# Turned tokens copied behind a block's last first product, gating in one Silu pass, and a moved step of weight additions

## The chip, the cores and the metric

The kernel runs on one core of one Trainium2 chip. The metric is the device time of one execution in microseconds. The engines are named as in the profile: PE (matmuls; PEld its weight loads), DVE (vector engine), ACT (activations and copies), POOL (the general engine), and SP (issues most transfers). Each works through its own instructions in order and waits on the others by semaphores.

## The reference, cut to what matters

Three stages follow one another: pooled attention, a mixture of experts with a skip score, and a dense feed-forward stage with a SiLU gate. The change lies in the last one and in the last expert work ahead of it.

```python
def _moe2_ref(x, w_in, w_out):          # x: 4608 x 512, w_in: 512 x 2048, w_out: 2048 x 512
    h = x @ w_in
    g = h * (1.0 / (1.0 + np.exp(-h)))
    return (g @ w_out).astype(np.float32)
```

## The kernel before, in words

Every fp32 operand of a matmul is split into a high half and a low half (a rounded copy, made by ACT, and what is left of it, a subtraction on DVE or POOL). A product is high x high, high x low and low x high, so 12 matmuls of 128x512 make one 128x512 product over a depth of 512.

The 4608 tokens of the feed-forward stage are nine blocks of 512. Three blocks are done plainly, in four **visits** (`visits` in `ffn`): visit 0 takes the first block with the hidden slices f = 0 to 5 (`HALF` = 6), visit 1 the second block with f = 0 to 15, visit 2 the first block again with f = 6 to 15, and visit 3 the third block with f = 0 to 15. The other six blocks are done in pairs by Strassen's scheme, in 24 steps n (`strassen(n)`, then `second(n - 1)`).

Inside a visit PE's order is `mm1(0)`, `mm1(1)`, `mm2(0)`, `mm1(2)`, `mm2(1)`, and so on: `mm1(f)` is the **first product** (into the PSUM tile `fh`), `mm2(f)` the **second product** (into `fop`). At a visit's end `mm2(last)` follows `mm2(last - 1)` with no first product between, and then the next visit's `mm1(0)` comes. Between `mm1(f)` and `mm2(f)` stand: a Sigmoid on ACT (`fsg`), a multiplication on DVE (`fsg` again), the high half on ACT (`fgh`), and the low half on DVE (`fgl`). The second product uses `fgh` in its first 8 matmuls and `fgl` in its last 4; the last one of a visit asks for `fgl` in every third.

The tokens of a block reach PE like this. `load_x` has SP load them into `fx` (four transfers), `turn(b, k)` transposes quarter k on DVE into `xt` (k = 0 to 3), and `xtrans(b, k)` splits `xt` into the halves of `xth` and `xtl` (ACT copies, DVE subtracts). Both halves lie in the tile `w1l`, which the profile therefore names; the last expert's first products read the same tile. So `xtrans` of a block can only run once all first products of the block ahead are done. For the first block the same is done out of `raw1` by way of `xn`, inside `moe`, between the last expert unit's second products (`yp`). This place is called the **handover** here.

Beside this, DVE decodes the weights of later slices (`convert`, up to three of its steps behind each first product, by the list `PACE`; DVE names `ft`, `fr`), ACT and POOL split them (`fh`, `fl`), and only then SP loads the next raw weights (`fr`). In visits 2 and 3 a generator `adds` makes the sums of weights that Strassen's scheme needs: per pair of slices one step of six POOL additions (`sw`), and one step with an ACT copy and a POOL subtraction (`shl`). One step is put behind each first product.

What fixes the order on an engine is the order of the calls in the code; no scheduler moves them. Every instruction goes through a helper at L115, so all have that line in the profile and are told apart by their tiles.

## Time and profile before

| | us |
|---|---|
| median of 3 runs | 1280.05 |
| lowest and highest of the 3 | 1272.41, 1280.28 |
| the profiled execution: its time | 1275.63 |
| the profiled execution: span from first to last instruction | 1273.9 |
| PE busy | 1227.5 |
| DVE busy | 874.7 |
| ACT busy | 565.7 |
| POOL busy | 357.0 |

The feed-forward stage begins at 504 us of the span and fills the rest. A matmul's end is modelled in the profile, so the busy share of PE says little; what PE loses is read from the starts: matmuls that follow each other at a steady distance lose nothing, and a larger distance is a wait. The profiled execution took 1.7 us more than its span, and lies between the three timed runs.

### The profile page before, as it was taken

The page shows a single profiled execution, that of the slowest core. Times are in us where ns is not written, and L with a number is a line of the kernel's source. Part 1 is how long each engine was busy: PE and PEld are TensorE (multiplying, and loading weights), DVE is VectorE, ACT ScalarE, POOL GpSimd, SP SyncE. Part 2 cuts the span into 40 slices and gives each one's busy share as a digit, 9 for nine tenths or more (in the row PEclk, how much of TensorE's full clock was granted, in tenths as well). Part 3 has the DMA queues.
Part 4 walks back from the last instruction along what each step waited for, and adds up shares of the span by engine and source line. Part 5 has one row for each costly group of instructions (what it writes and reads, how often), then busy time and mean ns, then how long its engine had stood idle before and what let it go on. Part 6 is the DMA issues. An engine that isn't in the chain of part 4 may idle for free.

```text
span 1273.9 us, 19902 instructions
## 1 busy us (share of the span) xinstructions
PE 1227.5 (96%) x6309; PEld 1041.7 (82%) x6310; DVE 874.7 (69%) x1599; ACT 565.7 (44%) x1200; POOL 357.0 (28%) x313
## 2 busy tenths in 40 slices
PE   6999898999999989999999999999999999999998
PEld 5988778998788977788887887788888888888887
DVE  6888876676776768899725365657785577846565
ACT  5877534455554544444433225433444233442321
POOL 5477532132222321322376512110201011110100
PEclk9999999999999999999999999999999999999999
DMA  9988536565666634568672435572565644362532
GB/s 374 327 300 290 193 104 242 172 199 179 236 211 207 192 109 116 141 177 296 237 238 110 132 91 131 192 205 101 182 172 200 163 143 155 137 228 93 180 118 89
DMA packets 110509, 234.45 MB, mean 184 GB/s; under 512 B 15525, under 2 KB 48421, under 8 KB 106720
## 3 DMA queue, kind: packets, MB, share of 16 engines
q1 hardware_dynamic: 103136, 216.47, 51.8%
q0 software_dynamic: 7008, 16.80, 4.2%
q8 instruction: 42, 0.69, 0.2%
q14 instruction: 35, 0.29, 0.1%
q10 hardware_dynamic: 288, 0.20, 0.1%
HBM read 183.24 MB, written 52.89 MB: 185 GB/s over the span
## 4 chain that ended last, share of the span: by engine, by line
PE 58%; DVE 3%; DMA 1%; ACT 1%; issue 0%; SPq 0%; DVEq 0%; ACTq 0%
PE yb L115 20%; PE ps L115 17%; PE fh L115 9%; PE fop L115 9%; PE hp L115 1%; DVE w1l L115 1%; DMA fx<-xa 1%; DMA wout<-wdo 0%; DVE st L115 0%; PE yp L115 0%; DVE xcb L115 0%; DVE fr L115 0%; DMA out<-fo 0%; DVE fsg L115 0%; ACT fgh L115 0%
## 5 line engine op out<-in xcount | busy, mean ns | idle before, releaser
L115 PE MATMUL yb<-wout,g 128*128 128x512 f32 x1152 | 265.3, 389 | 1.1 <-DMA wout<-wdo 1.1
L115 PEld LDWEIGHTS yb<-wout,g 128*128 128x128 f32 x1152 | 216.1, 188 | 46.6 <-DMA wout<-wdo 1.9
L115 POOL TENSOR_TENSOR tm<-tm,tm 128x512 f32<-128x512 f32 x24 | 32.2, 1340 | 404.8 <-ACT tm L115 404.8
L115 DVE TENSOR_TENSOR yacc<-yb,yacc 128x512 f32<-128x512 f32 x168 | 115.5, 687 | 29.0 <-PE yb L115 23.3
L115 ACT COPY tm<-ps 128x512 f32<-128x512 f32 x72 | 42.3, 587 | 142.7 <-PE ps L115 139.7
L115 ACT CAST g<-sg 128x512 fp32r<-128x512 f32 x96 | 59.7, 622 | 81.4 <-DVE sg L115 81.4
L115 PE MATMUL fh<-w1l,fh 128*128 128x512 f32 x336 | 85.5, 394 | 5.7 <-DVE w1l L115 3.0
L115 DVE TENSOR_TENSOR w2l<-raw,w2h 128x512 fp32r<-128x512 f32 x96 | 65.8, 690 | 28.8 <-ACT w2h L115 24.7
L115 ACT ACTIVATE hh<-hp 128x256 fp32r<-128x256 f32 (+1 forms) x96 | 39.4, 410 | 99.0 <-PE hp L115 88.3
L115 DVE TENSOR_TENSOR tm<-ps,tm 128x512 f32<-128x512 f32 x24 | 16.6, 691 | 97.3 <-PE ps L115 97.3
L115 PE MATMUL yp<-w2h,hh 128*128 128x512 f32 x208 | 82.9, 399 | 0.1
L115 PE MATMUL yp<-w2l,hh 128*128 128x512 f32 x208 | 81.2, 391 | 1.5 <-DVE w2l L115 1.5
L115 PE MATMUL yp<-w2h,hl 128*128 128x512 f32 x208 | 81.3, 391 | 0.0
L115 PEld LDWEIGHTS fh<-w1l,fh 128*128 128x128 f32 x336 | 63.6, 190 | 20.6 <-DVE w1l L115 4.1
L115 PE MATMUL hp<-xth,w1h 128*128 128x256 f32 (+2 forms) x384 | 72.3, 309 | 7.5 <-PEq L1663 3.6
L115 DVE TENSOR_TENSOR fsg<-fh,fsg 128x512 f32<-128x512 f32 x48 | 32.9, 686 | 67.6 <-ACT fsg L115 67.6
L115 PE MATMUL hp<-xtl,w1h 128*128 128x256 f32 (+2 forms) x384 | 72.4, 309 | 3.1 <-DVE xtl L115 1.9
L115 ACT ACTIVATE fsg<-fh 128x512 f32<-128x512 f32 x48 | 28.7, 598 | 96.1 <-PE fh L115 96.1
L115 PE MATMUL hp<-xth,w1l 128*128 128x256 f32 (+2 forms) x384 | 71.1, 308 | 0.0
L115 ACT ACTIVATE prb<-s,mx 128x72 f32<-128x72 f32 x288 | 65.3, 355 | 10.4 <-DVE mx L115 10.4
L115 DVE TENSOR_TENSOR g<-sg,g 128x512 fp32r<-128x512 f32 x96 | 65.7, 685 | 5.2 <-ACT g L115 4.7
L115 PEld LDWEIGHTS hp<-xth,w1h 128*128 128x128 f32 x384 | 60.1, 191 | 10.3 <-issue 8.7
(235 smaller groups left out, 2735.6 us busy)
## 6 DMA issues: line engine op xcount, KB each, us to landing
raw<-w SPq DMA_DIRECT2D x88, 512.0 KB, 4.8
wout<-wdo SPq DMA_DIRECT2D x48, 512.0 KB
win<-wdi SPq DMA_DIRECT2D x36, 512.0 KB
w1l<-wdi SPq DMA_DIRECT2D x36, 512.0 KB
xa<-x SPq DMA_DIRECT2D x36, 256.0 KB
fx<-xa SPq DMA_DIRECT2D x36, 256.0 KB
v<-vR SPq DMA_DIRECT2D x7, 1280.0 KB
fr<-w_in SPq DMA_DIRECT2D x16, 512.0 KB
```

The source lines that it names most:

```text
L115: ins = f(*a, **k)
```

## The change

It has three parts.

1. **Turned tokens.** At the end of a visit, quarters 0 and 1 of the next block are turned one first product earlier than before (behind the third-last, not the second-last), and quarters 2 and 3 too (behind the second-last, not the last). All four are split right behind the last first product; before, two were split there and two between the matmuls of the visit's last second product. At the handover the four quarters are turned and split ahead of the second products' evictions, through three buffers in place of two.
2. **Gating.** The Sigmoid on ACT and the multiplication on DVE become one Silu on ACT, in the visits (48 times) and in Strassen's steps (4 per step, 96 times).
3. **Additions.** `adds` takes no step behind the last first product of visit 2, and two steps behind the third one of visits 2 and 3. `PACE` gets one more entry, a 0 for the last slice of visit 1.

```diff
--- before.py
+++ after.py
@@ -45,7 +45,7 @@
 DEEP = 3
 LOW1 = 30, 31, 32, 35
 FMIN = float(np.uint32(0x38100000).view(np.float32))
-PACE = [3, 3, 3, 3, 1, 0] + [3, 2, 3] * 5
+PACE = [3, 3, 3, 3, 1, 0] + [3, 2, 3] * 5 + [0]
 HALF = 6
 POOL = 8
 PAD = 352
@@ -1066,19 +1066,18 @@
                 some(OPS[f // 2])
             gt = gates()
             one = s1.tile([1, 1], F32, name="one", tag="one")
-            nc.scalar.activation(one, gt[0:1, 0:1], AF.Sigmoid)
+            nc.scalar.activation(one, gt[0:1, 0:1], AF.Silu)
             sc = None
 
-            def xtrans(ks):
-                for k in ks:
-                    o = xn[:, k % 2, 0:DM]
-                    self.turn(o, x, k)
-                    self.split(self.fxh[:, k], self.fxl[:, k], o)
+            for k in range(5):
+                if k < 4:
+                    self.turn(xn[:, k % U, 0:DM], x, k)
+                if k:
+                    self.split(self.fxh[:, k - 1], self.fxl[:, k - 1], xn[:, (k - 1) % U, 0:DM])
 
             for s in (2, 1):
                 mm2(s, gt)
                 sc = scatter(s, sc, self.sq)
-                xtrans((4 - 2 * s, 5 - 2 * s))
                 while done:
                     f = done.pop(0)
                     self.ffn_conv3(f)
@@ -1213,8 +1212,7 @@
                         nc.tensor.matmul(ps, w[:, 0, P * k:P * (k + 1)], x[:, k], start=(i == 0), stop=(i == 11))
                         i += 1
                 sg = s2.tile([P, 512], F32, name=f"fsg{b}_{f}", tag="fsg")
-                nc.scalar.activation(sg, ps, AF.Sigmoid)
-                nc.vector.tensor_tensor(sg, ps, sg, ALU.mult)
+                nc.scalar.activation(sg, ps, AF.Silu)
                 gh = s2.tile([P, 512], F32R, name=f"fgh{b}_{f}", tag="fgh")
                 gl = s2.tile([P, 512], F32R, name=f"fgl{b}_{f}", tag="fgl")
                 nc.scalar.copy(gh, sg)
@@ -1227,7 +1225,7 @@
                     next(conv, None)
                 return gh, gl
 
-            def mm2(f, g, ops, fs, between=None):
+            def mm2(f, g, ops, fs):
                 h, l = self.fw[f]
                 gh, gl = g
                 last = f == fs[-1]
@@ -1237,8 +1235,6 @@
                                      start=(first and f == fs[0]), stop=(stop and last))
 
                 for s in range(4):
-                    if between and s in (1, 2):
-                        between(s + 1)
                     mm(s, gh, h, first=True)
                     mm(s, gh, l)
                     if last:
@@ -1410,10 +1406,7 @@
 
                 def sig(j, h):
                     sg[j] = s2.tile([P, DM], F32, name=f"sg{n}_{j}", tag="fgl" if j == 1 else "fsg")
-                    nc.scalar.activation(sg[j], h, AF.Sigmoid)
-
-                def gate(j, h):
-                    nc.vector.tensor_tensor(sg[j], h, sg[j], ALU.mult)
+                    nc.scalar.activation(sg[j], h, AF.Silu)
 
                 def high(j):
                     g[j] = slot(18 + 4 * (n % 2) + j, F32R, f"g{n}_{j}")
@@ -1441,33 +1434,23 @@
                 early(2)
                 prod(pa, a12, "b21", False)
                 sig(0, pa)
-                gate(0, pa)
                 prod(pb, s_4, "b22", False)
                 sig(3, h22)
                 h12 = h(1, "fgh")
                 nc.vector.tensor_tensor(h12, pb, p1, ALU.add)
                 high(0)
                 low(0)
-                gate(3, h22)
                 prod(pc, a22, "t4", False)
                 h21 = h(2, "fgl")
                 nc.vector.tensor_tensor(h21, pc, p1, ALU.add)
                 sig(1, h12)
                 high(3)
 
-                def t0():
-                    gate(1, h12)
-                    sig(2, h21)
-
                 def t1():
                     low(3)
                     high(1)
 
-                def t2():
-                    gate(2, h21)
-                    high(2)
-
-                return [t0, t1, t2, lambda: low(1), lambda: low(2)]
+                return [lambda: sig(2, h21), t1, lambda: high(2), lambda: low(1), lambda: low(2)]
 
             ring = [0]
 
@@ -1509,21 +1492,22 @@
                 for f in fs:
                     g[f] = mm1(b, f, pace.pop(0) if pace else 2)
                     if v >= 2:
-                        next(adds, None)
+                        for _ in range(0 if f == fs[-1] and v == 2 else 2 if f == fs[0] + 2 else 1):
+                            next(adds, None)
                     if v >= 1 and f > fs[0] + 2:
                         for k in [next(keeps, None)]:
                             if k is not None:
                                 self.ffn_keep(k)
                     if f == fs[0] + 2:
                         load_x(after if after is not None else doubles[0][0])
-                    if after is not None and fs[-1] - f in (0, 1):
-                        for k in (2, 3) if f == fs[-1] else (0, 1):
+                    if after is not None and fs[-1] - f in (1, 2):
+                        for k in (2, 3) if f == fs[-1] - 1 else (0, 1):
                             turn(after, k)
                     if f == fs[0] + 4 and fs[0] > 0:
                         load_part()
                     if f == fs[-1] and after is not None:
-                        xtrans(after, 0)
-                        xtrans(after, 1)
+                        for k in range(4):
+                            xtrans(after, k)
                     if f > fs[0]:
                         mm2(f - 1, g.pop(f - 1), ops, fs)
                     if after is None:
@@ -1550,7 +1534,7 @@
                     load_in(1)
                     tail = strassen(0)
                     load_x(doubles[1][0])
-                mm2(fs[-1], g.pop(fs[-1]), ops, fs, (lambda k: xtrans(after, k)) if after is not None else None)
+                mm2(fs[-1], g.pop(fs[-1]), ops, fs)
                 store(b, ops, fs)
             load_out(0)
 
```

DVE at the handover (`gt` is the gate of the last expert unit, `x_84<-yp` its evictions, `raw_79` the loaded tokens, `xn` the turned ones, `w1l` their low half, `fr_2602` raw weights), before:

```order
L115 RECIPROCAL gt<-gt 128x3
L115 SCALAR_TENSOR_TENSOR x_84<-yp_3694,gt,xr 128x512
L115 STREAM_TRANSPOSE xn<-raw_79 128x512
L115 TENSOR_TENSOR w1l<-xn,w1l 128x512
L115 STREAM_TRANSPOSE xn<-raw_79 128x512
L115 TENSOR_TENSOR w1l<-xn,w1l 128x512
L115 SCALAR_TENSOR_TENSOR raw_79<-fr_2602,raw_79 128x1024
L115 SCALAR_TENSOR_TENSOR fr_2602<-fr_2602,raw_79 128x1024
L115 SCALAR_TENSOR_TENSOR fr_2602<-raw_79,fr_2602 128x1024
L115 SCALAR_TENSOR_TENSOR x_84<-yp_3737,gt,xr 128x512
L115 STREAM_TRANSPOSE xn<-raw_79 128x512
L115 TENSOR_TENSOR w1l<-xn,w1l 128x512
```

and now:

```order
L115 RECIPROCAL gt<-gt 128x3
L115 STREAM_TRANSPOSE xn<-raw_79 128x512 x2
L115 TENSOR_TENSOR w1l<-xn,w1l 128x512
L115 STREAM_TRANSPOSE xn<-raw_79 128x512
L115 TENSOR_TENSOR w1l<-xn,w1l 128x512
L115 STREAM_TRANSPOSE xn<-raw_79 128x512
L115 TENSOR_TENSOR w1l<-xn,w1l 128x512 x2
L115 SCALAR_TENSOR_TENSOR x_84<-yp_3706,gt,xr 128x512
L115 SCALAR_TENSOR_TENSOR raw_79<-fr_2602,raw_79 128x1024
L115 SCALAR_TENSOR_TENSOR fr_2602<-fr_2602,raw_79 128x1024
L115 SCALAR_TENSOR_TENSOR fr_2602<-raw_79,fr_2602 128x1024
L115 SCALAR_TENSOR_TENSOR x_84<-yp_3743,gt,xr 128x512
```

The four turns and the four subtractions now stand ahead of the first eviction; before, two of each stood behind it, and two behind the second.

DVE at the end of visit 0 (the first number in `fgl_4_...` is f, that in `xt_0_...` is k), before:

```order
L115 SCALAR_TENSOR_TENSOR fr_3774<-fm,fr_3774 128x1024
L115 TENSOR_TENSOR fsg_4_4000<-fh_4_3987,fsg_4_4000 128x512
L115 TENSOR_SCALAR ft<-fr_3920 128x1024
L115 TENSOR_TENSOR fgl_4_4004<-fsg_4_4000,fgh_4_4003 128x512
L115 STREAM_TRANSPOSE xt_0_4016<-fx_0_3927 128x512
L115 STREAM_TRANSPOSE xt_1_4018<-fx_0_3927 128x512
L115 TENSOR_TENSOR fsg_5_4045<-fh_5_4032,fsg_5_4045 128x512
L115 TENSOR_TENSOR fgl_5_4049<-fsg_5_4045,fgh_5_4048 128x512
L115 STREAM_TRANSPOSE xt_2_4052<-fx_0_3927 128x512
L115 STREAM_TRANSPOSE xt_3_4054<-fx_0_3927 128x512
L115 TENSOR_TENSOR w1l<-xt_0_4016,w1l 128x512
```

and now:

```order
L115 SCALAR_TENSOR_TENSOR fr_3774<-fm,fr_3774 128x1024
L115 STREAM_TRANSPOSE xt_0_3971<-fx_0_3924 128x512
L115 STREAM_TRANSPOSE xt_1_3973<-fx_0_3924 128x512
L115 TENSOR_SCALAR ft<-fr_3917 128x1024
L115 TENSOR_TENSOR fgl_4_4003<-fsg_4_4000,fgh_4_4002 128x512
L115 STREAM_TRANSPOSE xt_2_4015<-fx_0_3924 128x512
L115 STREAM_TRANSPOSE xt_3_4017<-fx_0_3924 128x512
L115 TENSOR_TENSOR fgl_5_4047<-fsg_5_4044,fgh_5_4046 128x512
L115 TENSOR_TENSOR w1l<-xt_0_3971,w1l 128x512
L115 TENSOR_TENSOR w1l<-xt_1_3973,w1l 128x512
```

The multiplications are gone, and each pair of turns stands ahead of the low half `fgl` that it followed.

ACT at the end of visit 2, before:

```order
L115 ACTIVATE fsg_14_5122<-fh_14_5109 128x512
L115 CAST fgh_14_5125<-fsg_14_5122 128x512
L115 ACTIVATE fsg_15_5165<-fh_15_5152 128x512
L115 CAST fgh_15_5168<-fsg_15_5165 128x512
L115 CAST shl_5172<-sw_5129 128x1024
L115 CAST w1l<-xt_0_5136 128x512
L115 CAST w1l<-xt_1_5138 128x512
L115 CAST w1l<-xt_2_5176 128x512
L115 CAST w1l<-xt_3_5178 128x512
```

and now:

```order
L115 ACTIVATE fsg_14_5103<-fh_14_5090 128x512
L115 CAST fgh_14_5105<-fsg_14_5103 128x512
L115 CAST shl_5109<-sw_5067 128x1024
L115 ACTIVATE fsg_15_5142<-fh_15_5129 128x512
L115 CAST fgh_15_5144<-fsg_15_5142 128x512
L115 CAST w1l<-xt_0_5074 128x512
L115 CAST w1l<-xt_1_5076 128x512
L115 CAST w1l<-xt_2_5113 128x512
L115 CAST w1l<-xt_3_5115 128x512
```

The copy `shl` has moved from behind `fgh_15` to behind `fgh_14`; the four `w1l` copies now follow `fgh_15`.

## Rows read from the trace of the kernel before

**Rows 1.** The page, part 1: busy us, share of the span, instructions of each engine.

```profile
PE 1227.5 (96%) x6309; PEld 1041.7 (82%) x6310; DVE 874.7 (69%) x1599; ACT 565.7 (44%) x1200; POOL 357.0 (28%) x313
```

**Rows 2.** Waits of PE, 480 to 900 us: total us, times, longest.

```profile
PE fh L115 <- ACT w1l L115: 2.7, 2, 1.5
PE fop L115 <- ACT fgh L115: 1.4, 1, 1.4
...
PE fh L115 <- DVE w1l L115: 3.0, 3, 1.2
...
PE ps L115 <- ACT tm L115: 1.5, 1, 1.5
```

**Rows 3.** Timeline of PE at the handover: start us, duration us, [idle before].

```profile
504.47 0.61 PE L115 MATMUL fh<-w1l,fh 128*128 128x512 f32 x2
...
511.86 2.00 PE L115 MATMUL fh<-w1l,fh 128*128 128x512 f32 x8
```

**Rows 4.** Timeline of DVE ahead of the handover.

```profile
493.79 0.75 DVE L115 SCALAR_TENSOR_TENSOR x<-yp,gt,xr 128x512 f32<-128x512 f32 x1 [2.35 <-PE yp L115]
494.46 0.70 DVE L115 STREAM_TRANSPOSE xn<-raw 128x512 f32<-128x512 f32 x1
495.85 0.69 DVE L115 TENSOR_TENSOR w1l<-xn,w1l 128x512 fp32r<-128x512 f32 x1 [0.69 <-ACT w1l L115]
```

**Rows 5.** Timeline of ACT, same stretch.

```profile
490.83 1.28 ACT L115 ACT_TABLE_LOAD   x1
...
507.64 0.62 ACT L115 CAST w1l<-xn 128x512 fp32r<-128x512 f32 x1 [1.38 <-DVE xn L115]
```

**Rows 6.** Groups by line and form: busy us, mean ns of one, idle before.

```profile
L115 DVE TENSOR_TENSOR fsg<-fh,fsg 128x512 f32<-128x512 f32 x48 | 32.9, 686 | 67.6 <-ACT fsg L115 67.6
...
L115 ACT ACTIVATE fsg<-fh 128x512 f32<-128x512 f32 x48 | 28.7, 598 | 96.1 <-PE fh L115 96.1
```

**Rows 7.** Timeline of PE at the end of visit 0.

```profile
536.36 0.39 PE L115 MATMUL fop<-fh,fgh 128*128 128x512 f32 x1
...
538.17 1.07 PE L115 MATMUL fop<-fh,fgl 128*128 128x512 f32 x4
...
543.72 1.52 PE L115 MATMUL fh<-w1l,fh 128*128 128x512 f32 x6
```

**Rows 8.** Timeline of DVE, same end.

```profile
538.02 1.30 DVE L115 STREAM_TRANSPOSE xt<-fx 128x512 f32<-128x512 f32 x2 [1.30 <-DMA fx<-xa]
...
542.41 2.46 DVE L115 TENSOR_TENSOR w1l<-xt,w1l 128x512 fp32r<-128x512 f32 x4
```

**Rows 9.** Timeline of SP's queue, same end.

```profile
528.29 2.92 SPq L115 DMA_DIRECT2D fx<-xa  x4
```

**Rows 10.** Timeline of ACT, visit 0, third first product.

```profile
522.00 0.62 ACT L115 CAST fgh<-fsg 128x512 fp32r<-128x512 f32 x1 [1.10 <-DVE fsg L115]
```

**Rows 11.** Timeline of PE at the start of visit 3.

```profile
685.39 1.32 PE L115 MATMUL fh<-w1l,fh 128*128 128x512 f32 x5
...
691.98 1.30 PE L115 MATMUL fh<-w1l,fh 128*128 128x512 f32 x5
```

**Rows 12.** Timeline of DVE, same place.

```profile
684.03 6.63 DVE L115 TENSOR_TENSOR w1l<-xt,w1l 128x512 fp32r<-128x512 f32 x4
```

**Rows 13.** Timeline of POOL, same place.

```profile
674.80 2.54 POOL L115 TENSOR_TENSOR sw<-fh,fl 128x512 f32<-128x512 f32 x2
677.42 3.28 POOL L115 TENSOR_TENSOR sw<-sw 128x256 f32<-128x256 f32 x4
683.20 2.41 POOL L115 TENSOR_TENSOR shl<-sw,shl 128x1024 fp32r<-128x1024 f32 x1 [2.50 <-ACT shl L115]
685.69 3.28 POOL L115 TENSOR_TENSOR sw<-fh,fl 128x512 f32<-128x512 f32 x2
```

**Rows 14.** Timeline of ACT, same place.

```profile
681.55 0.62 ACT L115 CAST fgh<-fsg 128x512 fp32r<-128x512 f32 x1 [0.76 <-DVE fsg L115]
```

**Rows 15.** Timeline of ACT, second Strassen step.

```profile
792.75 0.58 ACT L115 COPY tm<-ps 128x512 f32<-128x512 f32 x1 [3.01 <-DMA out<-fo]
```

## The prediction

> **What bounds the kernel now.** I read the busy times first: PE is busy for 96% of the span [rows 1], so only what PE loses in waits can be won, not what DVE, ACT or POOL spend. A steady PE starts one 128x512 matmul every 0.227 us: the 8 matmuls from 536.36 to 538.17 took 1.81 us [rows 7]. So 12 of them, one product, take 2.72 us. The list of PE's waits came next. From the feed-forward stage on it is short [rows 2]: two waits for `w1l` from ACT (2.7 us) at the handover, one for `fgh` (1.4 us) at the end of visit 0, three for `w1l` from DVE (3.0 us) at the start of visit 3, and one for a copied Strassen product (1.5 us). Last I read the timelines around these four places, and took from the starts of the matmuls what each costs in full, slow restart included:
>
> - Handover: 12 matmuls from 504.47 to 511.86 [rows 3], 7.39 us where 2.72 are due: 4.67 lost.
> - End of visit 0: 24 matmuls from 536.36 to 543.72 [rows 7], 7.36 for 5.44: 1.92 lost.
> - Start of visit 3: 12 matmuls from 685.39 to 691.98 [rows 11], 6.59 for 2.72: 3.87 lost.
> - Second Strassen step: 1.5 lost [rows 2].
>
> Together 12.0 us, 0.9% of the time. This is the ceiling of what the three edits can give where they bear on PE.
>
> **The change, part by part.**
>
> *Handover.* DVE evicts a second product (493.79), then turns and splits two quarters, and does the other two only behind the next eviction [rows 4]. So the last copy of `w1l` starts at 507.64 [rows 5], 3 us after PE asked for the first. In the change the turns stand ahead of the evictions, where DVE was idle for 2.35 us [rows 4]. The tokens have landed, since nothing but the eviction held the first turn. ACT is free when its table load ends, 490.83 + 1.28 = 492.1 [rows 5]. Four turns of 0.70 and four subtractions of 0.69 [rows 4] are 5.6 us on DVE, so all halves stand by some 492.1 + 5.6 = 497.7, 6.8 us ahead of 504.47. What is pushed back is the first eviction, by some 4 us: behind it wait the scatter on POOL and the decoding of slice 3, which PE asks for five products after 504.47; nothing on PE waits for the evicted bank at once. Gain: the whole 4.67. If this cover failed, the first thing late would be that slice's weights.
>
> *Silu.* Per slice one DVE multiplication of 0.69 us goes, and ACT's Sigmoid of 0.60 becomes a Silu [rows 6]. No row shows a Silu. Its bounds are the Sigmoid's 0.60 and the 1.29 of both passes that it replaces; I take 0.60, the same engine, shape and source. In steady visits and in Strassen's steps the gate is not what PE waits for (no such wait in [rows 2] but at one visit's end), so 33 us of DVE work in the visits [rows 6], and more in Strassen's steps, are worth nothing by themselves. The gate counts only where a later step hangs on it, below.
>
> The Trainium skill speaks against this edit in one case (ScalarE: Activation LUTs, section Table sets): functions come in named sets, and a switch between sets is a load. One load took 1.28 us here [rows 5]. The same section lists copies and the like in every set. If Silu's set lacked the copy, each product would pay two loads; this is a rival below.
>
> *End of visit 0.* PE waited for `fgh`, and that hung on two turns that waited until 538.02 for the loaded tokens `fx` [rows 8], issued at 528.29 [rows 9], 9.7 us before. Now `fgh` needs no DVE, so this wait goes. But the turns have moved forward by one product pair, and the load has not: DVE now stands at the first turn with `fgl_4` and then `fgl_5` queued behind, and PE waits for those. How early is the load? It is issued when POOL and ACT have freed a weight buffer, a chain that begins with `fgh` of the third slice, which waited 1.10 us for the multiplication [rows 10]. Without it, the load is some 1.0 us earlier against PE and lands at 537.0 on the old clock. Two turns (1.30, [rows 8]), one decoding step (taken like a turn, 0.65) and `fgl_4` (0.7) end at 539.6. PE wants `fgl_4` at 538.17 [rows 7]: 1.4 lost. Then two more turns and `fgl_5` end at 541.5; PE, restarted at 539.6, wants it 6 matmuls later, at 541.0: 0.5 more. So 1.9 to 2.0 are lost in place of 1.92: the wait moves from `fgh` to `fgl`, and this end gives 0. Bounds: a load that lands 2 us sooner loses nothing (gain 1.9), one that lands 2 us later costs 2 more.
>
> *Start of visit 3.* Four subtractions took 6.63 us [rows 12], against 2.46 for the same four at the end of visit 0 [rows 8]. Beside them POOL ran `shl` until 685.61 and then `sw` [rows 13]. In the change nothing stands between `fgh_15` and the copies of `w1l`: `fgh_15` was at 681.55 and waited 0.76 for the multiplication [rows 14], the `shl` copy behind it is gone, and the turns are done one product earlier. So DVE can start the subtractions at about 682.2 instead of 684.03. Alone they would end at 684.7, ahead of 685.39 when PE begins. But the pause holds only in the program: POOL's six `sw` additions follow `shl` at once (685.61 to 685.69, [rows 13]), since they wait for no product. With `shl` one product (5.4 us) earlier, they run from about 680 to 686 (2.54 + 3.28, [rows 13]), beside the subtractions again. Bounds for one subtraction: 0.62 alone, 1.66 as in [rows 12]. I take 1.15, since it is the short additions of 0.82 that remain by then: the last ends at 682.4 + 4.6 = 687.0, and PE wants it at 685.39 + 7 x 0.227 = 687.0. Gain 3.4, with 0.5 left for slips; bounds 1.5 and 3.87.
>
> The Trainium skill (SBUF — State Buffer, Who interferes with whom) says that a DVE operation with two SBUF inputs and a GpSimd operation that reads SBUF fully block each other. By that rule each subtraction would wait through one 0.82 addition and end at 688.4: gain 2.5 in place of 3.4.
>
> *Strassen.* The copy that PE waits for waits itself for the outgoing blocks `fo` (3.01 us, [rows 15]). One multiplication stood on DVE ahead of their evictions; without it they leave 0.6 us earlier. Gain 0.6. The new entry of `PACE` does nothing: the list grants 53 steps and `convert` has 48. Two additions steps at once let ACT wait for POOL once in each of visits 2 and 3; `fgh` is wanted there 5.4 us after its first product, so this is hidden.
>
> **Sum**, on the profiled execution of 1275.6: 4.67 + 0 + 3.4 + 0.6 = 8.7, so 1266.9. That execution is 4.4 below the median of the three runs, which spread over 7.9. The mean of all four is 1277.1; I set the prediction on it: 1268.4.
>
> **The rivals** (times on the profiled execution).
>
> - *All cover holds*: the load comes in time at the end of visit 0, and POOL doesn't meet the subtractions. 4.67 + 1.92 + 3.87 + 0.6 = 11.1, so 1264.5. For it: it needs 2 us of luck in one transfer. Against it: nothing in the change moves that transfer by more than 1 us.
> - *The pause doesn't hold*: POOL's additions meet the subtractions in full, or the load slips by 2 us. 5 to 7 gained: about 1269.5. For it: [rows 12, 13].
> - *Table loads*: two loads per product. `fgh` would come 2.6 us later; PE has room but at visit ends, where some 1.2 us would be lost each time: about 1270.5. Against: the built order shows no further load among ACT's instructions.
> - *Slower*: the turn waits at the head of DVE at the end of visit 0. Each us that `fx` lands later is a us of PE. The load must land 8.7 us later than I reckon, near 546 on the old clock, before the gains are eaten: 1276 and above. Against: it took 9.7 us beside a load of weights, and would have to take 18.
>
> **How the numbers follow.** Forecast 0.60, all cover 0.15, the pause fails 0.18, table loads 0.02, slower 0.05. A median of runs that spread by 0.6% can tell about 1% (12.8 us) from no change. The forecast is 0.68% faster, so within it; with the spread, some 0.10 of its 0.60 and 0.06 of the 0.15 fall beyond 1%, so faster 0.16, slower 0.03, within 1% 0.81. The range: from the all-cover case on the lowest run (1272.4 - 11.1 = 1261.3, and 1 for its spread) to the failing pause on the highest (1280.3 - 6 = 1274.3, and 2 for the slower case's part): 1260 to 1276.
>
> **What would show it.** In the changed profile PE should run through the handover without a wait. At the end of visit 0 a wait of 1 to 2 us should stand for `fgl` in place of `fgh`, with DVE idle before `xt` until `fx` lands, for some 4 us. At the start of visit 3 the waits for `w1l` should be under 1 us in sum, with `sw` on POOL beside the subtractions. Silu should take 0.60 us. DVE's busy time should fall by about 99 us (144 x 0.686, [rows 6]) with nothing to show for it. The prediction is wrong if a Silu takes over 1.3 us, if the load lands beyond 540, or if the late evictions hold up PE at the start of visit 0.

## The result, and the profile after

| | kernel before | changed kernel |
|---|---|---|
| median of the runs timed side by side, us | 1276.49 (4 runs) | 1260.89 (4 runs) |
| lowest and highest | 1272.41, 1280.28 | 1258.69, 1262.43 |
| the profiled execution: time, span | 1275.63, 1273.9 | 1262.43, 1260.7 |

The ratio is 0.9877, with a 95% interval from 0.9833 to 0.9921: faster by 1.2%. Timed again later, the changed kernel took 1264.29 against 1277.29 for the kernel before, 0.9892 (0.9861 to 0.9923).

The busy times come first (the page, part 1: busy us, share, instructions); they answer to [rows 1].

```profile
PE 1225.5 (97%) x6309; PEld 1043.4 (83%) x6310; DVE 794.1 (63%) x1455; ACT 559.4 (44%) x1200; POOL 363.8 (29%) x313
```

PE does the same matmuls in a span that is 13.2 us shorter, so what was won is idle time of PE, and with it the slower matmuls that followed one wait (the granted clock was 0.50 from 508 to 511 us in the kernel before). The 80.6 us that DVE no longer works are no measure of it. The list of PE's waits from 480 to 900 us (total us, times, longest) was five lines long in the kernel before, of which [rows 2] shows four. Now it has two:

```profile
PE fop L115 <- DVE fgl L115: 1.2, 1, 1.2
PE fh L115 <- DVE w1l L115: 0.3, 1, 0.3
```

**Handover.** PE's timeline (start, duration, [idle before]) answers to [rows 3]: 12 matmuls from 503.63 to 506.35, which is 2.72 us, with no wait.

```profile
503.63 1.98 PE L115 MATMUL fh<-w1l,fh 128*128 128x512 f32 x8
505.44 1.07 PE L115 MATMUL fh<-w1l,fl 128*128 128x512 f32 x4
506.35 0.84 PE L115 MATMUL fh<-w1l,fh 128*128 128x512 f32 x3
```

DVE's timeline ahead of it answers to [rows 4]. The turns begin at 490.61, the last two subtractions end at 495.94, 7.7 us ahead of PE, and the eviction `x<-yp` stands behind them.

```profile
490.61 1.31 DVE L115 STREAM_TRANSPOSE xn<-raw 128x512 f32<-128x512 f32 x2
...
494.48 1.46 DVE L115 TENSOR_TENSOR w1l<-xn,w1l 128x512 fp32r<-128x512 f32 x2
495.86 0.74 DVE L115 SCALAR_TENSOR_TENSOR x<-yp,gt,xr 128x512 f32<-128x512 f32 x1
```

The eviction that was pushed back held up nobody: PE has no wait before 530.

**Silu.** The group of the visits' activations (busy us, mean ns of one, idle before; the second line is the group of ACT's table loads) answers to the Sigmoid of [rows 6]: 599 ns against 598. ACT loads its tables twice in the whole program, as before.

```profile
L115 ACT ACTIVATE fsg<-fh 128x512 f32<-128x512 f32 x48 | 28.7, 599 | 124.7 <-PE fh L115 124.5
...
L115 ACT ACT_TABLE_LOAD x2 | 2.6, 1283 | 1.6 <-PEq L1643 1.6
```

**End of visit 0.** PE's timeline, to set beside [rows 7]; the second line is the start of visit 1:

```profile
533.96 1.21 PE L115 MATMUL fop<-fh,fgl 128*128 128x512 f32 x4 [1.16 <-DVE fgl L115]
...
538.15 1.98 PE L115 MATMUL fh<-w1l,fh 128*128 128x512 f32 x8
```

DVE's timeline, beside [rows 8], and SP's queue, beside [rows 9]:

```profile
531.43 1.30 DVE L115 STREAM_TRANSPOSE xt<-fx 128x512 f32<-128x512 f32 x2 [3.95 <-DMA fx<-xa]
...
533.22 0.68 DVE L115 TENSOR_TENSOR fgl<-fsg,fgh 128x512 fp32r<-128x512 f32 x1
```

```profile
521.61 2.19 SPq L115 DMA_DIRECT2D fx<-xa  x4
```

The load of the next tokens is issued at 521.61, and DVE stands idle for 3.95 us until it has landed, at 531.43, 9.8 us later. The first `fgl` waits behind two turns and one decoding step, and PE for that: 1.16 us of idle time, 1.43 lost with the slow restart. Six matmuls later, at 535.75, PE waits again, for the `fgl` of the visit's last slice, and loses 0.4 there. Together 1.88 are lost.

**Start of visit 3.** PE's, DVE's and POOL's timelines, to set beside [rows 11], [rows 12] and [rows 13]. The four subtractions take 5.21 us in place of 6.63, still beside POOL's `sw`, but they start a good 3 us ahead of PE; only the last is late, by 0.25.

```profile
679.59 1.75 PE L115 MATMUL fh<-w1l,fh 128*128 128x512 f32 x7
681.59 0.50 PE L115 MATMUL fh<-w1l,fh 128*128 128x512 f32 x1 [0.25 <-DVE w1l L115]
```

```profile
676.32 5.21 DVE L115 TENSOR_TENSOR w1l<-xt,w1l 128x512 fp32r<-128x512 f32 x4
```

```profile
674.56 3.00 POOL L115 TENSOR_TENSOR sw<-fh,fl 128x512 f32<-128x512 f32 x2
677.64 4.50 POOL L115 TENSOR_TENSOR sw<-sw 128x256 f32<-128x256 f32 x4
```

**Strassen's entry.** This place surprised me. Here the rows of the kernel before are new. `hs` is the profile's name for the sums `h22`, `h12` and `h21` of a step, and the first one that DVE makes is `h12`. DVE's timeline, and SP's queue, before:

```profile
786.22 0.69 DVE L115 TENSOR_TENSOR hs<-ps,tm 128x512 f32<-128x512 f32 x1 [3.83 <-PE fop L115]
...
788.63 1.28 DVE L115 COPY fo<-fop 128x512 f32<-128x512 f32 x2
```

```profile
789.34 4.03 SPq L115 DMA_DIRECT2D out<-fo  x5
793.46 0.90 SPq L115 DMA_DIRECT2D wout<-wdo  x2
```

The same of the changed kernel:

```profile
772.98 0.69 DVE L115 TENSOR_TENSOR hs<-ps,tm 128x512 f32<-128x512 f32 x1 [2.13 <-ACT sg L115]
...
774.86 0.69 DVE L115 COPY fo<-fop 128x512 f32<-128x512 f32 x1
```

```profile
775.57 5.16 SPq L115 DMA_DIRECT2D out<-fo  x5
780.83 0.90 SPq L115 DMA_DIRECT2D wout<-wdo  x2
```

Measured from the first matmul of Strassen's step 0 (774.01 before, 764.46 after), DVE's addition `hs` comes at 8.53 us and not at 12.21, the first outgoing block leaves at 11.12 and not at 15.33, and the load of `wout` is issued at 16.38 and not at 19.45. In the kernel before the addition waited 3.83 us for the matmuls of visit 3's last second product, with which it has nothing to do. PE then waited for `tm` [rows 2] and, which the prediction left out, for `wout`, by the fifth line of that list of waits:

```profile
PE yb L115 <- DMA wout<-wdo: 1.1, 2, 0.8
```

**What each place loses.** The tables below are worked out from the starts of the matmuls: from a place's first to its last, less 0.2267 us for each between. "Handover" takes the first 24 matmuls of the stage, "visit 0" its last 24 and the 12 after them, "visit 3" 24 on either side of its start, "Strassen" the way from its first product to the 40th matmul behind the first `yb`, and "between" all other stretches from the handover to Strassen's start.

| lost, us | handover | end of visit 0 | start of visit 3 | Strassen's entry | between | sum |
|---|---|---|---|---|---|---|
| before | 4.69 | 1.92 | 3.89 | 3.65 | 0.63 | 14.8 |
| changed | 0.00 | 1.88 | 0.55 | 0.00 | 0.00 | 2.4 |

The difference is 12.4; the other 0.8 of the 13.2 is that the stage began at 503.63 and not at 504.47, ahead of anything that the change touches: 0.4 of it stands there at 459 us and all of it at 475. In the fourteen traces of this document the stage begins between 501.6 and 510.6 us, though ahead of the handover the kernels do not differ. So part of a difference between times comes from ahead of the stage, and the tables leave that part out.

### The profile page after: what moved, and what is told of

Read it like the earlier page. It is cut to its first block, busy times and chain, and to the rows that moved or that the text cites. A ratio compares the mean times of both kernels' runs of the same rounds, so it can differ in the third digit from the quotient of the medians.

```text
span 1260.7 us, 19778 instructions
## 1 busy us (share of the span) xinstructions
PE 1225.5 (97%) x6309; PEld 1043.4 (83%) x6310; DVE 794.1 (63%) x1455; ACT 559.4 (44%) x1200; POOL 363.8 (29%) x313
## 4 chain that ended last, share of the span: by engine, by line
PE 57%; DVE 2%; DMA 1%; issue 1%; POOL 0%; ACT 0%; SPq 0%; POOLq 0%; DVEq 0%
PE yb L115 21%; PE ps L115 18%; PE fh L115 9%; PE fop L115 9%; DMA xa<-x,sq 1%; DMA fx<-xa 1%; PE hp L115 0%; DVE w1l L115 0%; DVE w2l L115 0%; DVE hl L115 0%; POOL w1h L115 0%; DVE raw L115 0%; POOL fl L115 0%; SPq L115 0%; DVE fr L115 0%
## 5 line engine op out<-in xcount | busy, mean ns | idle before, releaser
L115 DVE TENSOR_TENSOR fgl<-fsg,fgh 128x512 fp32r<-128x512 f32 x48 | 41.4, 862 | 105.5 <-ACT fgh L115 105.4
L115 ACT ACTIVATE prb<-s,mx 128x72 f32<-128x72 f32 x288 | 65.3, 353 | 10.8 <-DVE mx L115 10.6
L115 PE MATMUL fop<-fh,fgh 128*128 128x512 f32 x168 | 65.4, 389 | 0.0
```

The costliest lines, as they stand in the source:

```text
L115: ins = f(*a, **k)
```

## The experiments

All times are medians; a kernel with one run has no interval. The kernel before was timed beside each group of them: 1283.37 beside e1, e2, e3 and e6, 1276.56 beside e4, e5 and e7, 1277.29 beside c1, c2 and e8, 1279.65 (one run) beside e9 and e10. So small differences are read from the traces.

| lost, us | handover | end of visit 0 | start of visit 3 | Strassen's entry | between |
|---|---|---|---|---|---|
| before again (c1) | 4.91 | 3.79 | 5.46 | 3.23 | 0.57 |
| changed again (c2) | 0.00 | 2.25 | 1.15 | 0.00 | 0.00 |
| handover only (e1) | 0.00 | 1.79 | 6.77 | 3.35 | 0.95 |
| Silu only (e2) | 4.81 | 0.00 | 4.74 | 0.00 | 0.00 |
| held buffer (e3) | 0.01 | 1.50 | 0.64 | 1.61 | 3.72 |
| additions back (e4) | 0.00 | 1.87 | 4.72 | 0.03 | 0.01 |
| early load (e5) | 0.00 | 0.00 | 1.11 | 0.29 | 0.00 |
| own buffer (e6) | 4.86 | 5.10 | 3.91 | 0.33 | 1.35 |
| late turns (e7) | 0.00 | 0.00 | 1.11 | 0.02 | 0.00 |
| both ends (e8) | 0.00 | 0.00 | 0.00 | 0.00 | 0.00 |
| held buffer, 64 bytes (e9) | 0.00 | 1.85 | 0.57 | 1.40 | 4.53 |
| shifted buffers (e10) | 0.01 | 1.58 | 0.67 | 0.54 | 3.72 |

**Each kernel a second time.** No edit: the kernel before (c1), and the changed one (c2).

> The kernel before, unchanged, profiled a second time. Theory: the four losses are of the program, so they return: 4.7 us at the handover, 1.9 at the end of visit 0, 3.9 at the start of visit 3, 3.65 at Strassen's entry, each within 1 us. Rival: how much a wait costs changes from execution to execution, because the granted clock falls behind some waits (mean clock 0.66 from 690 to 700 us in e1_handover_only, where the start of visit 3 cost 6.77): then one of the places costs 1.5 to 4 us more than in the first profile, with a granted clock under 1 just behind it.

> The changed kernel, unchanged, as the yardstick for e8_both_ends on the same chip. Both theories: 0.985 to 0.992 of the kernel before, losses of 0, 1.9, 0.6 and 0 us at the four places.

c1 took 1280.46 us (one run) and lost 18.0 us, 3.2 more than in its first profile. The waits themselves are nearly the same (1.6 in place of 1.4 for `fgh`, 2.7 and 3.0 for `w1l` as before). What differs is what follows them. The windows of c1 (busy us and instructions of PE, PEld, DVE, ACT, POOL, then the granted clock, DMA share, GB/s) behind the handover's wait, behind visit 0's, and in a steady stretch:

```profile
510.00:514.00 4.00, 4.00 (x11) 3.17 (x12) 1.28 (x2) 2.19 (x3) 2.83 (x2) 0.57 0.00 0
544.00:547.00 3.00, 3.00 (x9) 2.27 (x8) 3.00 (x7) 1.80 (x3) 0.00 (x0) 0.53 0.89 327
600.00:640.00 40.00, 40.00 (x177) 32.90 (x177) 31.88 (x34) 18.01 (x26) 15.62 (x10) 1.00 0.70 257
```

A mean near 0.5 is the lower of the two levels, 1.2 in place of 2.4 GHz; matmuls then start 0.427 us apart and not 0.227. In the first profile of the kernel before the clock fell behind the handover alone (0.50 from 508 to 511). So the waits are of the program, as the theory had it, but "each within 1 us" failed at two of the four places, and the rival holds there: what a wait costs depends on whether the clock falls behind it. c2 took 1264.29 (0.9892), lost 3.4 us, and its clock stayed up.

**Handover only (e1).** The kernel before, with the first part of the change alone.

```diff
-            def xtrans(ks):
-                for k in ks:
...
+            for k in range(5):
+                if k < 4:
+                    self.turn(xn[:, k % U, 0:DM], x, k)
+                if k:
+                    self.split(self.fxh[:, k - 1], self.fxl[:, k - 1], xn[:, (k - 1) % U, 0:DM])
...
-                xtrans((4 - 2 * s, 5 - 2 * s))
```

> The kernel before, with the handover's turns and splits ahead of the second products' evictions and nothing else of the change. My theory: the whole stall goes, 4.7 us, at this one place; the end of visit 0 (1.9 lost), the start of visit 3 (3.9 lost) and the entry to Strassen's steps (3.2 lost, as read from the starts of its matmuls) stay as they were; time -0.37%. Rival: DVE is late with what was pushed back (evictions, decoding of slice 3), and part of the 4.7 us comes back as waits for weights in visit 0; then the gain is 2 to 3 us.

It took 1274.83 against 1283.37, 0.9934 (0.9912 to 0.9956), by times more than the 0.37% that I expected. The handover's loss is gone and the other places have theirs. The start of visit 3 costs 6.77 here, with the same waits as before (3.0 us in three), because the clock fell behind them (0.66, the last but two column):

```profile
690.00:700.00 10.00, 8.31 (x23) 6.32 (x24) 5.96 (x9) 1.81 (x3) 4.07 (x5) 0.66 0.36 118
```

**Silu only (e2).** The kernel before, with the second part alone.

```diff
-                nc.scalar.activation(sg, ps, AF.Sigmoid)
-                nc.vector.tensor_tensor(sg, ps, sg, ALU.mult)
+                nc.scalar.activation(sg, ps, AF.Silu)
...
-                    nc.scalar.activation(sg[j], h, AF.Sigmoid)
+                    nc.scalar.activation(sg[j], h, AF.Silu)
...
-                gate(0, pa)
...
-                gate(3, h22)
```

> The kernel before, with Silu in place of Sigmoid and multiplication, in the visits and in Strassen's steps, and the turns where they were. My theory, from the changed kernel's trace: the multiplication was the last reader of the Strassen tile h22, so that h12 had to take the buffer of fgh_15 and wait for the last second product, with the evictions fo, their transfers and the next weights queued behind it on DVE and SP. With Silu the entry to Strassen's steps loses nothing: 3.2 us gained there. At the end of visit 0 fgh_5 no longer stands behind the turns, and fgl_4 still stands ahead of them: under 0.5 lost in place of 1.9. Start of visit 3: fgh_15 is 0.7 earlier, 3.0 lost in place of 3.9. Sum 5 to 6 us. Rival, the account in the prediction: the multiplication's own 0.6 us is all that Strassen's entry gains, and the rest of what the changed kernel won there comes from its other parts (or from transfers that happened to be fast); then 2.5 or more are lost there still, and the sum is about 3 us.

It took 1272.78 against 1283.37, 0.9919 (0.9888 to 0.9950). The end of visit 0 and Strassen's entry lose nothing. So the edit that I had priced at 0.6 is worth the most of the three, 1.92 + 3.65 + 0.63 = 6.2 us by the first profile's losses (in the changed kernel the 1.92 is given back). At the end of visit 0 it loses nothing because the turns still stand at their old place, behind `fgl_4`. The start of visit 3 lost 4.74 and not the 3.0 that I expected: 3.1 by the waits (2.3 us in three, against 3.0 before) and their restarts, and 1.7 because the clock was at 0.50 from 695.2 to 698.6. In the times, the gains of e1 and e2 (8.5 and 10.6 us) add up to more than the whole change brought (15.6), so they can't be split up by times.

**Additions back (e4).** The changed kernel without its third part.

```diff
-                        for _ in range(0 if f == fs[-1] and v == 2 else 2 if f == fs[0] + 2 else 1):
-                            next(adds, None)
+                        next(adds, None)
```

> The changed kernel, with the additions stepping once behind each first product, as before. My theory: the shl copy stands ahead of the w1l copies again and its POOL subtraction beside the first DVE subtraction; fgh_15 is 0.7 earlier than in the kernel before and the turns are done, so the start of visit 3 loses 2 to 3.5 us in place of 0.5. Rival: Silu and the earlier turns brought the gain there, the moved step nothing: under 1 us lost.

It gave 1269.01 (one run). The start of visit 3 loses 4.72 and nothing else changes. PE's list of waits has there:

```profile
PE fh L115 <- DVE w1l L115: 2.3, 3, 1.2
```

Of the 4.72, 3.1 are the waits with their restarts, as in e2, and 1.6 are matmuls at a clock of 0.50, from 687.5 to 690.9. In the changed kernel the waits there are 0.3 us (0.7 in c2) and the clock stays up. So it is the third part, and not the earlier turns, that wins there: 1.9 us against c2 and 2.5 against the changed kernel's first profile by the waits alone, 3.6 and 4.2 with the fall of the clock in this execution.

**Strassen's entry: own buffer (e6).** The kernel before with all its multiplications; only the sum `h12` has a buffer of its own, in place of one of the two `fgh` buffers.

```diff
-                h12 = h(1, "fgh")
+                h12 = s1.tile([P, DM], F32, name=f"hs{n}_1", tag="h12")
```

> The kernel before, with a buffer of its own for h12 in Strassen's steps; Sigmoid and multiplication stay, and so do all other stalls. My theory: the entry to Strassen's steps no longer waits for the last second product's end, and takes 22 us in place of 24.7, with all multiplications still there; the page's wait of PE for the copied product is gone or under 0.5. Rival: as above, it stays within 0.5 us of 24.7.

It gave 1279.34 (one run). The loss at the entry falls from 3.65 to 0.33 although every multiplication is there. DVE's timeline, with Strassen's first matmul at 781.04; the first line is one of the multiplications, the second the addition into `h12`:

```profile
788.74 0.69 DVE L115 TENSOR_TENSOR sg<-ps,sg 128x512 f32<-128x512 f32 x1 [1.29 <-ACT sg L115]
789.40 0.69 DVE L115 TENSOR_TENSOR hs<-ps,tm 128x512 f32<-128x512 f32 x1
```

It no longer waits for PE: it starts 8.36 us in. `wout` is issued at 16.38, as in the changed kernel. What kept the time of this kernel up lies elsewhere: at the end of visit 0 the tokens landed at 543.03 and PE lost 5.10 us, again with a lower clock (0.83 from 540 to 550).

**Strassen's entry: held buffer (e3, e9), shifted buffers (e10).** The other way round: the changed kernel, where DVE reads one element of `h22` into a tile that nothing uses, as late as the multiplication read it. So `h22` holds its buffer, and `h12` must again take the other one. e3 has a tile of 4 bytes, e9 one of 64; e10 writes a tile of 4 bytes and reads nothing.

```diff
                 low(0)
+                if n == 0:
+                    late = s1.tile([1, 1], F32, name="late", tag="late")
+                    nc.vector.tensor_copy(late, h22[0:1, 0:1])
                 prod(pc, a22, "t4", False)
```

In e9 the tile is `[1, 16]`; in e10 the last added line is `nc.vector.memset(late, 0.0)`.

> The changed kernel, with one 1x1 copy on DVE that reads h22 behind h12 in the first Strassen step, so that h22's buffer is held as the multiplication held it. It adds under 0.2 us of DVE work. My theory: h12 waits for the last second product again, and the entry to Strassen's steps (first Strassen matmul to first yb matmul) takes some 24.5 us again in place of 21.8: 2 to 3 us lost. Rival: the multiplication's time on DVE counted, not the buffer: nothing is lost (21.8 to 22.0).

> e3_held_buffer again, with the small tile 64 bytes wide in place of 4: the buffers of the visits then lie 64 bytes further than in the changed kernel, and not 32 as in e3_held_buffer. Theory of the buffer: the first addition again waits for PE's last second product, some 12.3 us behind the first matmul of Strassen's first step, and 1 to 2.5 us are lost at the entry, so this part of e3_held_buffer stays. Theory of the address: the second products' matmuls start 0.227 us apart again (0.2335 in e3_held_buffer), so the 1.2, 0.7 and 1.3 us lost inside visits 1, 2 and 3 go. Rival: the slower matmuls were of that one execution or of the extra instruction; then they come back at 0.2335 here, or show at random.

> The changed kernel with a 4-byte tile ahead of the same buffers, which lie 32 bytes further by it, and one DVE write of that tile that reads nothing and holds no buffer. Theory of the address: the second products' matmuls start 0.2335 us apart as in e3_held_buffer, 1.2, 0.7 and 1.3 us are lost inside visits 1, 2 and 3. Theory of the buffer: nothing is lost at Strassen's entry, 21.8 us from its first product to the first yb, the first addition 8.5 us behind the first matmul. Rivals: the address does nothing (0.2267 and no loss in the visits); the extra DVE instruction itself delays the entry (24 us or a loss of over 1 us there).

e3 gave 1273.3, e9 1268.98, e10 1265.8 (one run each). DVE in e3, with Strassen's first matmul at 773.72:

```profile
786.01 0.69 DVE L115 TENSOR_TENSOR hs<-ps,tm 128x512 f32<-128x512 f32 x1 [5.89 <-PE fop L115]
...
787.22 0.13 DVE L115 COPY late<-hs 1x1 f32<-1x1 f32 x1
```

The addition waits for PE again and starts 12.29 us in, and 12.32 in e9 (12.21 in the kernel before, 8.54 in e10). So the cause of DVE's wait is the buffer: one read of one element brings it back. The built programs agree: `h12` lies where `h22` lay in the changed kernel, and where the visit's last `fgh` lay in the kernel before. But the loss that comes back is 1.61 and 1.40, some 1.0 when e10's 0.54 is taken off, and not 3.2 to 3.65. The multiplications without the held buffer lose 0.33 (e6), no more than e5, which has neither (0.29). What goes with the loss is the time at which SP issues `wout`, behind the outgoing blocks, counted from Strassen's first matmul:

| us | `hs` | first out | second out takes | `wout` issued | lost |
|---|---|---|---|---|---|
| before, c1, e1 | 12.21 | 15.33 to 15.34 | 1.74, 1.42, 1.51 | 19.45, 19.15, 19.24 | 3.65, 3.23, 3.35 |
| e3, e9 | 12.29, 12.32 | 14.85, 14.88 | 0.46, 0.38 | 17.70, 17.66 | 1.61, 1.40 |
| e6 | 8.36 | 11.59 | 0.36 | 16.38 | 0.33 |
| changed, c2, e2, e4, e7, e8 | 8.53 | 11.12 | 0.36 | 16.37 to 16.38 | 0.00 to 0.03 |
| e5, e10 | 8.53, 8.54 | 11.12, 11.15 | 0.36 | 16.38, 16.47 | 0.29, 0.54 |

The last rows show that up to 0.5 us is lost at the first `yb` products even when `wout` is issued at its early time. In the kernel before `wout` comes 3.07 us later than in the changed one. By the table that is 1.3 for the held buffer (17.70 against 16.38), 0.5 for the multiplication ahead of the evictions (15.33 against 14.85), which is the 0.6 of my prediction, and 1.3 for the second out, which takes 1.4 to 1.7 us of SP in place of 0.4 in all three executions that have both. It waits for ACT's eviction, but that had ended at 789.25 in the kernel before, and the issue ended at 791.53. What the traces show beside it is one 16 KB packet of the DMA queue that carries instructions: it is under way from 15.77 to 17.16 us in the kernel before, from 15.89 to 16.91 in c1 and from 15.70 to 16.93 in e1, and each time the second out ends 0.30 to 0.38 us behind the packet's end. In e3 and e9 the packet starts at 14.19 and 14.12, and the second out is hardly held; in the kernels of the last three rows it starts at 11.65 to 12.31, when SP still waits for an eviction. That the issue waits for the packet is read from these times and was not tested. If it does, this part of the delay hangs on where a load of instructions falls.

The second result of these runs I had not looked for. In e3 PE lost 3.72 us spread over all visits: the second products' matmuls started 0.2329 us apart and not 0.2267. In the built programs the `fgh` and `fgl` buffers, and all others of their pool (`fsg`, `sg`, `hs`, `tm`, `xt`, `fo`), lie 32 bytes further in e3 and e10 and 64 in e9; in e6 they lie 2048 further. e10 shows the same 3.72 us without holding anything, so neither the execution nor the held buffer is the cause. My theory that 64 bytes would undo it fell: e9 has 0.2335 and loses 4.53. e6 has 0.2269. Of these buffers PE reads `fgh` and `fgl` alone, and behind the entry to Strassen's steps, where it reads neither, its matmuls keep their distance in all kernels; but that it is these two that matter was not tested apart from the others. One group of PE (busy us, mean ns of one, idle before), in the changed kernel and then in e10:

```profile
L115 PE MATMUL fop<-fh,fgh 128*128 128x512 f32 x168 | 65.4, 389 | 0.0
```

```profile
L115 PE MATMUL fop<-fh,fgh 128*128 128x512 f32 x168 | 66.4, 395 | 0.0
```

**End of visit 0: early load (e5), late turns (e7).** The changed kernel; in e5 SP loads visit 1's tokens one first product earlier, in e7 the turns at the end of visit 0 stand where they stood before the change.

```diff
-                    if f == fs[0] + 2:
+                    if f == fs[0] + (1 if v == 0 else 2):
                         load_x(after
```

```diff
-                    if after is not None and fs[-1] - f in (1, 2):
-                        for k in (2, 3) if f == fs[-1] - 1 else (0, 1):
+                    if after is not None and fs[-1] - f in ((0, 1) if v == 0 else (1, 2)):
+                        for k in (2, 3) if f == fs[-1] - (v > 0) else (0, 1):
```

> The changed kernel, with the load of the next block's tokens in visit 0 put one slice earlier, so that SP issues it ahead of the weight load that waits for POOL. My theory: the tokens land some 8 us earlier, well ahead of the first turn, DVE doesn't wait, and the end of visit 0 loses under 0.2 us in place of 1.8: 1.7 us faster than the changed kernel, 1.35% faster than the kernel before. Rival: the load now waits for the last scatter of the expert stage and holds the weight load behind it, so decoding falls back and the loss turns up at a later slice.

> The changed kernel, with the turns of visit 0 where they were before (behind its last two first products), all else as changed. My theory: fgl_4 is no longer behind the wait for the tokens, and fgh_5 needs no DVE, so under 0.5 us are lost at the end of visit 0 in place of 1.8: the earlier turns cost there, they don't gain. Rival: the load's lateness itself is the bound, wherever the turns stand: 1.5 to 2 us lost, at the next visit's first product instead.

e5 gave 1262.92 (0.9888, 0.9867 to 0.9909), e7 1259.2 (one run). Both lose nothing at the end of visit 0. So the 1.9 us there belong to the turns that now wait for a load that did not move with them, as the prediction had it. In the times of e5 the 1.9 us can't be told: it is 1.1% faster than the kernel before, where I had expected 1.35%, and so no faster than the changed kernel.

**Both ends (e8).** The changed kernel with e7's edit, and with the double step of additions in visit 3 alone. POOL's last work in visit 2 is then a `sw` group that is done early, and the `shl` step behind it waits for a copy that stands in visit 3.

```diff
-                        for _ in range(0 if f == fs[-1] and v == 2 else 2 if f == fs[0] + 2 else 1):
+                        for _ in range(0 if f == fs[-1] and v == 2 else 2 if f == fs[0] + 2 and v == 3 else 1):
```

> The changed kernel with the turns of visit 0's end at their old place, and with the double step of additions in visit 3 alone, so that visit 2's last step on POOL is the six sw additions of the pair ahead, done before DVE subtracts, and the copy for shl stands in visit 3. Theory: the 1.9 us at the end of visit 0 and the 0.5 to 1.1 at the start of visit 3 go, 2.4 us under the changed kernel (1258.5 beside 1260.9, ratio to the kernel before 0.0019 lower). Each subtraction takes 0.62 us instead of 1.2. Rival: the subtractions are slowed by something else than POOL (the four copies on ACT that they follow, 0.62 each, or the memory traffic); then they still take 1.2 us and 0.5 to 1.1 us stay lost at the start of visit 3.

It gave 1259.35 (0.9863, 0.9835 to 0.9892), and beside it c2 1264.29. PE has no wait left from 480 to 900 us. DVE and POOL at the start of visit 3:

```profile
672.30 2.49 DVE L115 TENSOR_TENSOR w1l<-xt,w1l 128x512 fp32r<-128x512 f32 x4
```

```profile
666.90 3.26 POOL L115 TENSOR_TENSOR sw<-sw 128x256 f32<-128x256 f32 x4
680.85 2.39 POOL L115 TENSOR_TENSOR shl<-sw,shl 128x1024 fp32r<-128x1024 f32 x1 [10.68 <-ACT shl L115]
```

With POOL idle from 670.16 on, the four subtractions take 2.49 us against 5.21; the rival falls, since ACT's copies are the same. The times of e8 and c2 overlap (1257.95 to 1262.30, and 1259.03 to 1268.66), so that e8 is faster than the changed kernel is shown by the traces (3.4 us less lost than in c2), not by the times.

## Why the prediction was right or wrong

The time lay in the range, near its lower end, 7.5 us under the forecast. By the chances the less likely came: 0.81 stood on a change within 1% and 0.16 on a faster kernel, and the ratio is 0.9877, though its interval (0.9833 to 0.9921) includes 0.99. By its steps:

- **What bounds the kernel**: right. The gain is PE's waits, and e8 has none left from the handover to Strassen. The ceiling of 12.0 was too low: the same trace holds 14.8, and a second execution of the kernel before 18.0.
- **Handover, 4.67**: right, 4.69 to 0.00, from the cover that was named: the tokens were there, DVE was free from 490.6, and the eviction behind the turns held up nobody.
- **Silu at 0.60**: right (0.599). The Trainium skill (ScalarE: Activation LUTs, section Table sets) has a switch between table sets cost a load, and the prediction named two loads for each product as a rival; the trace has two in the whole program, as before.
- **DVE's busy time, 99 less**: it fell by 80.6. Other DVE work took longer, `fgl` among it; nothing waits for this but the places above, and I did not follow it up.
- **End of visit 0, nothing gained**: right in place and size, 1.92 to 1.88, and in its two waits, 1.4 and 0.5 reckoned and 1.4 and 0.4 measured. The wait moved from `fgh` to `fgl`, DVE stood idle for 3.95 us until the load landed, and e5 and e7 show that this is the earlier turn's own price. What I did not see is that the price was avoidable.
- **Start of visit 3, 3.4**: right, 3.34 (3.89 to 0.55), though 0.55 was the lucky side: the changed kernel lost 1.15 there in c2, and e5 and e7 lost 1.11. POOL's `sw` did run on beside the subtractions, of which the first took 1.79 us and the others 1.22, where 1.15 was taken for each. The Trainium skill (SBUF — State Buffer, section Who interferes with whom) has the two engines block each other. The trace bears that out: beside POOL four subtractions take 5.21 us and POOL's four additions 4.50; apart they take 2.49 and 3.26. The slower end that I drew from that rule, a gain of 2.5, did not come (688.4 there should read 688.2: four times 0.62 and 0.82 from 682.4).
- **Strassen, 0.6**: this is the step that failed: "One multiplication stood on DVE ahead of their evictions; without it they leave 0.6 us earlier." The place and the direction were right, the size was 3.65 (3.23 in c1). I counted the multiplication as an instruction of 0.6 us and not as the last reader of `h22`. With it there, `h12` had to take the buffer of the visit's last `fgh`, and so wait for PE's last second product, with the evictions, the outgoing blocks and the load of `wout` queued behind on DVE and SP. With Silu, `h22`'s last reader is ACT's activation, `h12` takes `h22`'s buffer, and its addition starts 3.7 us earlier. e6 takes the wait and the loss away with the multiplications kept. e3 and e9 put the wait back without them, and 1.4 to 1.6 us of the loss; the rest went with the multiplication ahead of the evictions and with the slow second out, whose cause was not tested. I also read 1.5 from one line of [rows 2] and passed over another of the same list, 1.1 us for `wout`.
- **Sum**: 8.7 forecast, 12.4 in the traces. 3.05 of the 3.7 is Strassen, the rest some small losses between the places that went with the multiplications (0.63, gone in e2).
- **From the profile to the median**: the medians differ by 15.6 and 13.0, the traces by 12.4 (first profiles) to 15.6 (c1 to the changed kernel, 18.0 less 2.4). The kernel before can pay more for its waits than its first profile shows, since the clock can fall behind several of them (three of the four places in c1). I had carried over the losses of one execution. What part of the difference between the medians comes from ahead of the stage, no run tells.

## What to carry to other kernels

When an edit takes an instruction away, list the buffers that it was the last to read, and see who takes those buffers next and what is queued behind that taker: here a multiplication of 0.69 us held one up for 3.7 us. When an edit moves a consumer forward, move its load by as much (1.9 us lost here, none with either undone). And price a wait of PE by several executions, since behind some of them the matmuls run on at half the clock.

## What I had not expected of the hardware

- The granted clock falls to about a half (0.50 to 0.57 in windows of 3 to 4 us) behind some of PE's waits and not behind others of the same length: the same three waits at the start of visit 3 (3.0 us) cost 3.89 us in one execution, 5.46 and 6.77 in two others.
- When a pool of buffers, PE's stationary operand of the second products among them, lay 32 or 64 bytes further in SBUF, these matmuls started 0.2329 and 0.2335 us apart in place of 0.2267, at the same duration of a weight load (188 ns); a shift by 2048 bytes did not do it (0.2269). The first products, whose operands did not move, kept nearly their distance at 32 bytes (0.2271) and less so at 64 (0.2291). What in the address matters is open.
- An issue on SP took 1.4 to 1.7 us in place of 0.4 in three executions, each time while a 16 KB packet of the instruction queue was under way, and ended 0.30 to 0.38 us behind it. Of 175 issues in the fourteen traces that began during such a packet, 88 ended 0.3 to 0.42 us behind it and 51 ahead of its end, so this is no rule yet.
- DVE and POOL, each on SBUF alone, took turns: a subtraction of 0.6 us took 1.2 beside POOL's additions, and these 1.18 in place of 0.73 to 0.74.
